# Reordering a kernel's prologue: four slab reads behind the last store, table work ahead of filter copies, a late constant

## The chip, the cores and the metric

The kernel runs on one core of a Trainium2 chip. The metric is device time per execution in microseconds (us), and a kernel's time is the median of its executions. Every profile shown here is one execution of the program, taken by the hardware profiler; times in it count from the start of its span, which is about 1.75 us shorter than the device time of the same execution.

## The reference, cut to what matters

```python
def _attn_ref(x, filt_r, filt_i):            # x: (8, 3008, 256)
    X = np.fft.rfft(x, axis=1)
    Y = X * (filt_r + 1j * filt_i)[None]     # filters: (1505, 256)
    return np.fft.irfft(Y, n=3008, axis=1)

def _moe_ref(x, w_gate, w_val, w_out):       # (24064, 256), d_ff 1536
    return (np.maximum(x @ w_gate, 0) * (x @ w_val)) @ w_out
```

## The kernel before

A spectral filter feeds a gated feed-forward. The transform of one batch goes in two steps. The first (psA) makes four slabs, which are stored to a DRAM buffer (Abuf) and read back in another order (at). The second (psX) multiplies the slabs by tables; its result is multiplied by the filters (tt and uu), transformed back (psD, Dbuf, dC, psY) and then used by the main stream: gate and value products (psG, psV), VectorE's product of the two, output products (psO). Batches from the second on are transformed between main-stream steps. Batch 0 has to be done before the main stream can begin: this is the prologue, about 60 us, and the change is in it.

```python
def load_at(b, c):                     # slab c back from DRAM, 768 rows of 512 B
    ...
    nc.sync.dma_start(ats[b][c:c + 125:4], _ap(Abuf[b], ...))
def make_back_t(q):                    # back table, PE then VectorE
    ...
        nc.vector.tensor_copy(I2t[:, 8 * q + e:8 * q + 8:2, :], psI[e])
def make_back_u(q):                    # second table out of the first
    nc.tensor.matmul(psI, swap, I2t[:, 8 * q:8 * q + 8, :], start=True, stop=True)
    nc.scalar.copy(I2u[:, 8 * q:8 * q + 8, :], psI)
def place_filter(fi, a, half, copy):   # 32 filter rows to their second place
    copy(dst[r + 32:r + 64, gs, :], dst[r:r + 32, gs, :])
def warm(n, cols=512):                 # filler matmuls on junk, to keep the clock up
    ...
# prologue
    load_x(0, nc.sync, ...)            # batch 0, 3 MB
    nc.sync.dma_start(WF, ...)         # fold table, first used for batch 2
    ...                                # filters: GpSimd's queue
    for i, f in enumerate(items_a(0)): # 16 psA items; every fourth ends in a store
        f()
        if i == 12:
            load_at(0, 0)
            load_at(0, 1)
    for c in range(2, 4):
        load_at(0, c)
    ...                                # filter copies, tables: see the diff
    for i in range(15):
        warm(2)
    load_x(1, nc.sync, ...)            # next batch, 3 MB
    first_b(amid)                      # psX, products, inverse of batch 0
```

In the timelines here the fillers and psX, and VectorE's filter copies and table evictions, run in the order in which the program gives them. In the profile before, psX starts at 36.16 us, as the last filler ends, and VectorE's first table eviction at 25.99 us, behind three filter copies that had waited for their rows until 23.06 us. So a filler that runs too long delays psX, and a waiting filter copy delays the tables.

Of the kernel before, what the change touches and what calls it, by code (L numbers as in the profile page):

```python
# [35 lines left out]
def _ap(t, offset_elems, ap_list):  # L36
    return dataclasses.replace(
        t, offset=t.offset + offset_elems, ap=[list(p) for p in ap_list]
    )
# [81 lines left out]
def kernel(  # L121
# [10 lines left out]
    nc = tc.nc  # L132
# [11 lines left out]
    wa_h, fold_h, f2_h, tab_h = _tables()  # L144
# [14 lines left out]
    WF = consts.tile([128, 4, 32], FP32)  # L159
# [11 lines left out]
    def load_x(b, eng, cols):  # L171
        w = NX2 * D
        for c, c0, c1 in cols:
            for m in range(3):
                rows = min(32, B * N1 - (b * N1 + 32 * m))
                eng.dma_start(XF[c][m:m + 4 * rows - 3:4, c0:c1],
                              _ap(x, (b * N1 + 32 * m) * N2 * D + c * w + c0,
                                  [[N2 * D, rows], [1, c1 - c0]]))
# [20 lines left out]
    def make_back_u(q):  # L199

        psI = ps.tile([128, 8, 64], FP32, tag=fft_tag(), name="psI")
        nc.tensor.matmul(psI, swap, I2t[:, 8 * q:8 * q + 8, :], start=True, stop=True)
        nc.scalar.copy(I2u[:, 8 * q:8 * q + 8, :], psI)

    def place_own():

        for i, t in enumerate((I2t, I2u)):
            o = 192 + i * 128
            nc.vector.tensor_copy(t[64:, NG - 2:, :],
                                  tabs[64:, o:o + 128].rearrange("p (g n) -> p g n", g=2))  # L210
        nc.vector.tensor_copy(M1, tabs[:NROW, 448:])
# [21 lines left out]
    def place_filter(fi, a, half, copy):  # L233

        dst = FILT[fi][1]
        gs = slice(H * half, H * half + H)
        r = a * 64
        copy(dst[r + 32:r + 64, gs, :], dst[r:r + 32, gs, :])

    def place_nyq():  # L240
        for (src, dst), n in zip(FILT, nyq):
            nc.vector.tensor_copy(dst[96:97, NG - 1, :], n)
# [20 lines left out]
    def fft_tag(side=False):  # L263
        if side and turn.get("side"):
            return turn["side"]
        turn["i"] += 1
        return turn["tags"][turn["i"] % len(turn["tags"])]

    def items_a(b):

        def one(c, j, st):
            if j == 0:
                st["asb"] = sb.tile([128, NC2 * D], BF16, tag="asb", bufs=4, name="asb")
            psA = ps.tile([128, 512], FP32, tag=fft_tag(True), name="psA")
            o = (c * NC2 % NX2) * D + j * 512
            nc.tensor.matmul(psA[0:NROW], WA, XF[c * NC2 // NX2][:, o:o + 512],
                             start=True, stop=True)
            dst = st["asb"][:NROW, j * 512:(j + 1) * 512]
            nc.scalar.copy(dst, psA[0:NROW])
            if j == 3:  # L280
                eng = nc.scalar if b and c > 1 else nc.sync
                eng.dma_start(_ap(Abuf[b], c * NROW * NC2 * D, [[NC2 * D, NROW], [1, NC2 * D]]),
                                  st["asb"][:NROW])
        for c in range(N2 // NC2):
            st = {}
            for j in range(NC2 * D // 512):
                yield lambda c=c, j=j, st=st: one(c, j, st)
# [59 lines left out]
    def load_at(b, c):  # L347
        if c == 0:
            ats[b] = sb.tile([128, NG, D], BF16, tag="at", bufs=1, name="at")
        nc.sync.dma_start(ats[b][c:c + 125:4],  # L350
                          _ap(Abuf[b], c * NROW * NC2 * D, [[D, 32], [4 * NC2 * D, NG], [1, D]]))
# [164 lines left out]
    def warm(n, cols=512):  # L516

        psJ = ps.tile([128, 512], FP32, tag=fft_tag(True), name="psJ")
        for i in range(n):
            nc.tensor.matmul(psJ[:, :cols], junk[:, 0:128], junk[:, :cols], start=True, stop=True)  # L520
# [12 lines left out]
    nc.vector.memset(XF[1][:, 0:2 * q], 0.0)  # L533
    nc.gpsimd.memset(XF[1][:, 2 * q:], 0.0)
    load_x(0, nc.sync, ((0, 0, q), (0, q, 2 * q), (0, 2 * q, 4 * q), (1, 0, 2 * q), (1, 2 * q, 4 * q)))
    nc.sync.dma_start(WF, nc.inline_tensor(fold_h, name="dft_fold").ap())
    for (src, dst) in FILT:
        nc.vector.memset(dst[64:128, NG - 2:, :], 0.0)
    load_own_filters()
# [4 lines left out]
    warm(11)  # L544
    for i, f in enumerate(items_a(0)):
        f()
        if i == 12:
            load_at(0, 0)
            load_at(0, 1)
    for c in range(2, 4):  # L550
        load_at(0, c)
    for half in range(2):
        for a in range(2):
            place_filter(0, a, half, nc.vector.tensor_copy)
    for i in range(3):
        make_back_t(i)
    warm(6)
    place_filter(1, 0, 0, nc.vector.tensor_copy)
    for i in range(3):
        make_back_u(i)  # L560
    place_own()
    for a, half in ((1, 0), (0, 1), (1, 1)):
        place_filter(1, a, half, nc.vector.tensor_copy)
    place_nyq()
    for i in range(15):
        warm(2)
    load_x(1, nc.sync, ((0, 0, 2 * q), (0, 2 * q, 4 * q), (1, 0, 4 * q)))

    early = items_a(1)

# [116 lines left out]
```

## Time and profile before

| what | value |
|---|---|
| time before, first three executions | 895.17 to 895.47 us, median 895.28 |
| the profiled execution | 896.64 us (span 894.9) |
| TensorE busy | 97% of the span |
| first forward product psX | 36.16 us |
| first product of the main stream (VectorE) | 63.63 us |

The lines themselves are in the prediction.

### The profile page before, as it was taken

What the parts mean: (1) busy time and instruction counts of PE and PEld (TensorE: products, weight loads), DVE (VectorE), ACT (ScalarE), POOL (GpSimd) and SP (SyncE); (2) the same over time, 40 slices, a digit from 0 to 9 for tenths busy, and PEclk for the clock granted to TensorE, in tenths of its full rate; (3) what the DMA queues carried; (4) which work ended last, traced back from release to release, by engine and by line L of the source; (5) the groups of instructions that cost most, each with busy time, mean ns of one, the idle gap of its engine ahead of it and who ended that gap; (6) DMA issues with size and microseconds to landing.
All of it is one profiled execution on the core that took longest, in us unless ns stands there. A gap on an engine that the chain in (4) does not pass through costs nothing.

```text
span 894.9 us, 19039 instructions
## 1 busy us (share of the span) xinstructions
PE 871.8 (97%) x7090; PEld 508.0 (57%) x7210; DVE 569.0 (64%) x873; ACT 499.4 (56%) x891; POOL 364.6 (41%) x361
## 2 busy tenths in 40 slices
PE   8899999999999999999999999999999999999997
PEld 2335555556556565556655565556655566666665
DVE  2737766577665776667765677657766577655553
ACT  4375565556555556555655565555565555555553
POOL 4350698038661386415672167802867000000001
PEclk9999999999999999999999999999999999999999
DMA  8997448534465335463365333763446512331111
GB/s 246 288 224 164 135 132 176 113 96 116 123 156 135 113 101 140 129 144 92 100 172 136 97 100 105 181 139 79 115 140 149 120 31 81 82 73 36 37 32 53
DMA packets 114099, 109.18 MB, mean 122 GB/s; under 512 B 20359, under 2 KB 98599, under 8 KB 113366
## 3 DMA queue, kind: packets, MB, share of 16 engines
q1 hardware_dynamic: 90294, 80.10, 34.8%
q0 software_dynamic: 22992, 26.41, 12.1%
q8 instruction: 57, 0.93, 0.5%
q10 hardware_dynamic: 720, 1.45, 0.4%
q14 instruction: 36, 0.29, 0.1%
HBM read 61.93 MB, written 49.81 MB: 125 GB/s over the span
## 4 chain that ended last, share of the span: by engine, by line
PE 85%; DVE 4%; ACT 4%; DMA 3%; issue 1%; POOL 1%; SPq 1%; POOLq 0%; ACTq 0%; DVEq 0%
PE psG L467 26%; PE psO L486 25%; PE psV L467 24%; DVE prod L472 3%; PE psF L323 3%; ACT vsb L470 3%; PE psD L394 2%; PE psX L364 2%; PE psY L451 2%; DMA at<-Abuf 1%; DMA Fti<-in_filt_i_dram 1%; PE psJ L520 1%; SPq L340 1%; ACT dsb L401 0%; DMA XF<-in_x_dram 0%
## 5 line engine op out<-in xcount | busy, mean ns | idle before, releaser
L472 DVE SCALAR_TENSOR_TENSOR prod<-psG,vsb 128x512 bf16<-128x512 f32 x564 | 388.8, 690 | 263.7 <-ACT vsb L470 257.8
L470 ACT CAST vsb<-psV 128x512 bf16<-128x512 f32 x564 | 332.1, 589 | 263.9 <-PE psV L467 180.3
L467 PE MATMUL psG<-yT,WgT 128*128 128x512 bf16 x1107 | 330.7, 379 | 6.9 <-DVE prod L472 0.8
L486 PE MATMUL psO<-WoT,prod 128*128 128x256 bf16 x2256 | 336.4, 273 | 1.1
L467 PE MATMUL psV<-yT,WvT 128*128 128x512 bf16 x1030 | 315.2, 380 | 0.8 <-ACT asb L330 0.5
L486 PEld LDWEIGHTS <-prod 128*128 128x128 bf16 x2256 | 220.6, 98 | 143.4
L467 PEld LDWEIGHTS <-WgT 128*128 128x128 bf16 x1128 | 110.0, 98 | 136.2 <-issue 3.3
L467 PEld LDWEIGHTS <-WvT 128*128 128x128 bf16 x1128 | 98.6, 98 | 41.8 <-issue 30.5
L258 POOL CAST scr<-prod 128x8 f32<-128x8 bf16 x24 | 4.6, 191 | 258.8 <-DVE prod L472 258.8
L509 POOL DMA_DIRECT2D out_dram<-osb x5 | 2.6, 536 | 195.9 <-ACT osb L499 195.9
L380 DVE TENSOR_TENSOR tt<-psX,Ftr 128x512 bf16<-128x512 f32 x96 | 65.0, 681 | 7.9 <-PE psX L364 7.9
L499 ACT COPY osb<-psO 128x512 f32<-128x512 f32 x92 | 53.9, 586 | 27.9 <-PE psO L486 27.3
L309 POOL TENSOR_TENSOR fold<-XP 128x1024 f32<-128x1024 f32 x24 | 56.5, 2356 | 20.5 <-PE psF L323 19.4
L380 DVE TENSOR_TENSOR uu<-psX,Fti 128x512 bf16<-128x512 f32 x89 | 60.4, 679 | 0.0
L401 ACT CAST dsb<-psD 128x512 bf16<-128x512 f32 x96 | 51.5, 589 | 12.1 <-PE psD L394 11.7
L296 POOL DMA_DIRECT2D XP<-in_x_dram x96 | 56.7, 596 | 3.2 <-PE psG L467 1.6
L310 POOL TENSOR_TENSOR XP<-XP 128x1024 f32<-128x1024 f32 x24 | 56.4, 2350 | 1.9
L330 ACT CAST asb<-psF 128x512 bf16<-128x512 f32 x48 | 25.8, 589 | 30.5 <-PE psF L323 30.5
L330 DVE CAST asb<-psF 128x512 bf16<-128x512 f32 x48 | 30.9, 686 | 18.6 <-PE psF L323 17.0
L456 ACT CAST yT<-psY 128x512 bf16<-128x512 f32 x47 | 27.6, 586 | 22.9 <-PE psY L451 22.7
L458 DVE CAST yT<-psY 128x512 bf16<-128x512 f32 x47 | 32.0, 680 | 9.8 <-PE psY L451 9.8
L451 PE MATMUL psY<-M,dC 96*128 96x94 bf16 (+18 forms) x604 | 37.5, 198 | 0.6 <-DMA dC<-Dbuf 0.5
(70 smaller groups left out, 494.0 us busy)
## 6 DMA issues: line engine op xcount, KB each, us to landing
at<-Abuf SPq DMA_DIRECT2D x32, 384.0 KB
dC<-Dbuf SPq DMA_DIRECT2D x64, 192.0 KB
XP<-in_x_dram POOLq DMA_DIRECT2D x48, 256.0 KB, 5.9
Dbuf<-dsb SPq DMA_DIRECT2D x23, 512.0 KB
XP<-in_x_dram POOLq DMA_DIRECT2D x96, 96.0 KB, 2.7
Abuf<-asb SPq DMA_DIRECT2D x96, 96.0 KB
out_dram<-osb SPq DMA_DIRECT2D x69, 94.0 KB
XF<-in_x_dram SPq DMA_DIRECT2D x15, 256.0 KB
```

Source lines behind the costliest of these rows:

```text
L296: nc.gpsimd.dma_start(xp[r:r + 24, 0:4:2, :], _ap(x, (b * N1 * N2 + o) * D, [[N2 * D, 24], [47 * N2 * D, 2], [1, 512]]))
L309: tt(t, xp[:, 0:2], xp[:, 2:4], op=ALU.add)
L310: tt(xp[:, 2:4], xp[:, 0:2], xp[:, 2:4], op=ALU.subtract)
L330: copy(asf[:, :, q, :], banks[q])
L380: nc.vector.tensor_tensor(p, psX, filt, op=ALU.mult)
L401: nc.scalar.copy(dsb[:, a, o:o + 2, :], psD[a])
L451: nc.tensor.matmul(psY[:, o:o + w], dCs[b, n2 // 8][:, n2 % 8, h * 128:(h + 1) * 128], M1[:, n1:n1 + w], start=True, stop=True)
L467: nc.tensor.matmul(pt[:, :W], w[:, h, ft * 128:(ft + 1) * 128], yt[:, h, :], start=(h == 0), stop=(h == 1))
L470: nc.scalar.copy(vsb, psV[:, :W])
L472: nc.vector.scalar_tensor_tensor(prod, in0=psG[:, :W], scalar=0.0, in1=vsb, op0=ALU.max, op1=ALU.mult)
L486: nc.tensor.matmul(psO[:, t % 2], prods[ft][:, t * 128:(t + 1) * 128], WoT[:, ft, :], start=(ft == 0), stop=(ft == NFT - 1))
L499: copy(osb[:, t0 % 2:t % 2 + 1], psO[:, t0 % 2:t % 2 + 1])
```

## The change

The intent is to have batch 0's slabs in SBUF sooner. Store 3 is to go out before any slab read, so that the last read can follow it earlier; the back tables are to be made before VectorE turns to filter copies that wait for transfers; ScalarE takes two of these copies; the fold table, needed much later, gives up its early place.

```diff
     load_x(0, nc.sync, ((0, 0, q), ...))
-    nc.sync.dma_start(WF, nc.inline_tensor(fold_h, name="dft_fold").ap())
...
     for i, f in enumerate(items_a(0)):
         f()
-        if i == 12:
-            load_at(0, 0)
-            load_at(0, 1)
-    for c in range(2, 4):
+    for c in range(4):
         load_at(0, c)
-    for half in range(2):
-        for a in range(2):
-            place_filter(0, a, half, nc.vector.tensor_copy)
     for i in range(3):
         make_back_t(i)
     warm(6)
-    place_filter(1, 0, 0, nc.vector.tensor_copy)
+    place_filter(0, 1, 0, nc.scalar.copy)
     for i in range(3):
         make_back_u(i)
+    for a, half in ((0, 0), (0, 1), (1, 1)):
+        place_filter(0, a, half, nc.vector.tensor_copy)
     place_own()
-    for a, half in ((1, 0), (0, 1), (1, 1)):
-        place_filter(1, a, half, nc.vector.tensor_copy)
+    for a, half, copy in ((1, 0, nc.scalar.copy), (0, 0, nc.vector.tensor_copy),
+                          (0, 1, nc.vector.tensor_copy), (1, 1, nc.vector.tensor_copy)):
+        place_filter(1, a, half, copy)
     place_nyq()
-    for i in range(15):
+    for i in range(14):
         warm(2)
     load_x(1, nc.sync, ...)
+    nc.sync.dma_start(WF, nc.inline_tensor(fold_h, name="dft_fold").ap())
```

## The prediction

> **What bounds the kernel now.** I read the page first: the busy shares and the chain that ended last.
>
> ```profile
> PE 871.8 (97%) x7090; PEld 508.0 (57%) x7210; DVE 569.0 (64%) x873; ACT 499.4 (56%) x891; POOL 364.6 (41%) x361
> ...
> PE 85%; DVE 4%; ACT 4%; DMA 3%; issue 1%; POOL 1%; SPq 1%; POOLq 0%; ACTq 0%; DVEq 0%
> ```
>
> TensorE is busy for 97% of the span and carries 85% of the chain. In order of time, the main stream (gate, value and output products) begins near 61.6 us and hardly pauses afterwards. The diff touches nothing of it: TensorE's instruction list differs only by two dropped filler matmuls in the prologue. So the change can move the time only by shifting the start of that stream, and everything is decided in the first 60 us. What the forward products of batch 0 (psX) wait for is the next view, the timeline of TensorE (start us, length us, engine, line, operation):
>
> ```profile
> 26.80 0.39 PE L202 MATMUL psI<-I2t,tabs 128*128 128x512 bf16 x1 [2.12 <-DVE I2t L197]
> 27.46 1.25 PE L202 MATMUL psI<-I2t,tabs 128*128 128x512 bf16 x2 [0.27 <-DVE I2t L197]
> 28.50 7.74 PE L520 MATMUL psJ<-junk 128*128 128x512 bf16 x30
> 36.16 0.41 PE L364 MATMUL psX<-at,F 64*64 64x256 bf16 x8
> ```
>
> Thirty filler matmuls run from 28.50 to 36.16 us and psX follows without a gap. Filler is meant to fill a wait; here it was itself the last thing waited for. The timeline of GpSimd, whose small copy reads all four slabs, says when the data was there:
>
> ```profile
> 35.16 0.18 POOL L258 CAST scr<-at 32x8 f32<-32x8 bf16 x1 [18.73 <-DMA at<-Abuf]
> ```
>
> The last slab landed by 35.16 us, so the filler cost 1.0 us. It ran late for two reasons. It stands behind the back tables, whose VectorE copies (25.99 us) stood behind four filter copies that waited for filter transfers. And the granted clock was 0.50 from 28 to 30 us (the stretches view): 30 matmuls took 7.74 us instead of the 6.5 us that 0.216 us each at full clock would give (the main stream's spacing: 0.43 us for two).
>
> Second, the slabs. The SyncE queue's timeline, and its waits (us in total, times, longest):
>
> ```profile
> 21.03 2.98 SPq L350 DMA_DIRECT2D at<-Abuf  x2
> 24.10 0.79 SPq L282 DMA_DIRECT2D Abuf<-asb  x1
> 26.32 5.84 SPq L350 DMA_DIRECT2D at<-Abuf  x2
> ```
>
> ```profile
> SPq L350 <- DMA Abuf<-asb: 8.5, 4, 4.6
> ```
>
> Each slab read waits for its own store to land. Store 3 is issued at 24.10 us, behind two reads, and read 3 waits 4.6 us for it, to 31.59 us. What the DMA engines did meanwhile is in their busy row for 32 to 34 us (40 slices of 0.05 us):
>
> ```profile
> DMA  0000000000000000000445698999877563689999
> ...
> DMA packets 489, 0.25 MB, mean 125 GB/s; under 512 B 1, under 2 KB 489, under 8 KB 489
> ```
>
> They were empty for nearly 1 us from 32 us. Counting packet time on the engines per microsecond, the idle part was about 0.58 us in 31 to 32, 0.96 us in 32 to 33 and 0.18 us in 33 to 34, together 1.7 us. From 17 to 31 us they are full. So the slabs' arrival is bound by DMA work plus this hole.
>
> **What the Trainium skill says.** "DMA: Bandwidth & Descriptors", section "Queues, rings and completion order": descriptors of one queue are consumed in ring order on each engine, and an engine takes turns between queues. The trace agrees: reads 0 and 1 are issued from 21.03 us, but their 512-byte packets appear only from 25.5 us, behind stores 1 and 2, in turn with the filters' packets of GpSimd's queue. Section "Anatomy of one DMA — SWDGE (gpsimd) path" puts most of the roughly 2 us fixed cost of a transfer into the receipt of the write; here store 3's last 4 KB packets run before 31 us and the queue is released at 31.59 us, which fits a smaller receipt. "TensorE: Matmul & The Clock Gate", Part 1: after an idle window of about 3.4 us the clock falls to half; the trace has one such window at half, 27.3 to 30.7 us, after 3.4 us in which TensorE was busy for about 1.2 us. "ScalarE: Activation LUTs", "Rules for kernel authors": about 0.3 us plus 0.83 ns per element, hence an estimated 2.85 us for a filter copy of 3072 elements on ScalarE, against 0.95 us on VectorE in this trace. No ScalarE copy of that size is in the trace to check it with; its 512-element ones take 0.58 us, slightly below the page's sum of 0.72.
>
> **The change part by part.**
>
> Slab reads behind store 3. The evictions of store 3's data end at 23.23 us, so it is issued at about 23.3 instead of 24.10. What matters more is the ring: reads 0 and 1 (768 packets of 512 bytes each at about 28 ns over 16 engines = 1.34 us each) no longer stand before it. It follows store 2, whose packets end at 25.5 us. Store 3 is 96 packets of 4 KB at 165 ns over 16 engines = 1.0 us of service; in turn with the filters, which last to about 28 us, nearer 2 us. It should land at about 28.3 us. By then three reads, 4.0 us of service, are queued, so read 3, issued at about 29 us, joins a full ring and the hole goes: -1.7 us.
>
> Fold table last. Its 64 KB come as 512-byte packets of 40 ns (112 were seen): 112 x 40 / 16 = 0.28 us less ahead of the slabs: -0.3 us. In its new place it is 0.3 us behind 3 MB of the next batch, and first used hundreds of microseconds later: 0. Its 0.6 us of issue on SyncE falls at about 35 us, where that queue idles until the first Dbuf store (44.70 before): 0.
>
> The last slab therefore lands at 35.1 - 1.7 - 0.3 = 33.1 us.
>
> Tables first. psI for them is ready from 22.54 to 23.28 us, the six VectorE copies take 2.08 us, so they end at about 25.3 instead of 28.07. Six fillers end at 24.7, the three table products at about 25.6, and 28 fillers x 0.216 = 6.0 us at full clock end at about 31.6. With TensorE nearly without a gap from 23.9 to 27.3 us the half-clock window of before should not come there. The filler is then off the path, and psX starts at about 33.2 us instead of 36.16: -2.9 us, of which 2.0 belong to the slabs and 0.9 to the filler.
>
> Filter copies. VectorE: tables to 25.3, three Ftr copies x 0.95 to 28.2, three small ones x 0.2 to 28.8, three Fti copies to 31.7, two Nyquist rows to 32.1. ScalarE: first copy 23.3 to 26.1 (its rows landed at 23.06), three table evictions to 28.0, second copy from 28.2 to 28.9 (the landing of Fti) to about 31.5. Both are ready before 33.2, by 1 us and more: 0 on the path.
>
> Afterwards psX, products, inverse, Dbuf stores and dC reads form a chain of engine and transfer lengths, 36.16 to 61.6 us, whose parts are unchanged; the next batch's 3 MB move earlier along with read 3. I expect it to shift as a whole. Nearly all of the 2.9 us should reach the end, as the main stream has no slack that waits for a fixed time. I take off 0.1 us for a clock loss described next. Sum: 895.28 - 2.8 = 892.5 us.
>
> **The rivals.** First, the clock falls later. TensorE now idles from about 31.6 to 33.2 us. In the window 30.7 to 34.1 us it would be busy about 0.9 us of filler plus 0.9 us of the first products, half of it; 35% was too little before, 67% (37.5 to 41) enough. A half-clock window from 34.1 would lengthen psX and fillers, but products there wait mostly for GpSimd's uu and VectorE, so 0.3 to 1 us: a time near 893.3. Chance about a third.
>
> Second, filters replace slabs. Store 3's 4 KB packets, in turn with the filters' 0.5 KB ones, delay the last filter rows by up to 0.8 us; if ScalarE's copy is slower too, the first uu waits until perhaps 33.5 to 34 us: a time of 893 to 893.5. For it: margins of 1 us only. Against: VectorE loses two of eight copies and the tables come first.
>
> Third, the hole does not close: store 3 crawls beside the filters and read 3 still arrives on an empty ring. Then only the filler's 1 us and the 0.3 us of the table remain: 894 us. Against: 4 us of reads stand behind store 3.
>
> Fourth, a larger gain: fillers were cut from 30 to 28, as if the slabs were expected by about 31.6 us. If stores land sooner with less queued, psX at 32.2 gives 891.4.
>
> **Range and chances.** The gain lies in the prologue and can hardly exceed 4.5 us or turn into a loss of over 1 us; 2% is 17.9 us. Range 891.2 to 894.0. Faster by over 2%: 0.01; within: 0.98; slower: 0.01.
>
> **What would show it.** Right: reads all after store 3 on the SyncE queue; the wait for it ending near 28.5; no empty DMA slices between 31 and 33 us; last slab landed near 33.1; filler over near 31.6, with no half clock at 28 to 30; psX near 33.2; the main stream 2.8 us earlier. Wrong: psX held by filler again, a product held by a filter copy on ScalarE, DMA idle before read 3, or a shift of psX that the Dbuf and dC transfers swallow.

## The result, and the profile after

The changed kernel took 894.21 us, the median of four executions from 893.26 to 895.10; the kernel before took 895.38 us in four. The ratio is 0.9987, with a 95% interval of 0.9970 to 1.0004. (A ratio is the mean time of one kernel's fast runs over that of the other's of the same rounds, so not quite the ratio of the medians.) The forecast was 892.5 us with a range up to 894.0. The medians moved in the forecast direction, by 1.2 us where 2.8 were forecast; this interval still includes no change; of the changed kernel's three, only that of the third call below does not. A difference within 2% had been given a chance of 0.98, and by that measure all runs count as the same.

The page's busy shares and chain of the changed kernel:

```profile
PE 875.7 (98%) x7208; PEld 506.8 (57%) x7208; DVE 567.1 (64%) x871; ACT 504.2 (57%) x893; POOL 364.4 (41%) x361
...
PE 93%; DMA 3%; ACT 1%; POOL 1%; issue 1%; DVE 0%; SPq 0%; ACTq 0%; POOLq 0%
```

TensorE carries 93% of the chain, against 85% before. TensorE's timeline where before the filler led straight into psX:

```profile
25.24 0.91 PE L202 MATMUL psI<-I2t,tabs 128*128 128x512 bf16 x3
25.99 6.21 PE L520 MATMUL psJ<-junk 128*128 128x512 bf16 x28
34.34 0.41 PE L364 MATMUL psX<-at,F 64*64 64x256 bf16 x8 [2.14 <-DMA at<-Abuf]
```

The table products come at once, without the waits for VectorE of before. The 28 fillers run at full clock and are over at 32.2 us, and psX waits 2.14 us for slabs. So the filler is off the path, but the slabs land at 34.3 us and not at 33.1. ("Land" here means the moment at which the waiting engine is released; the last packet runs about 0.6 us earlier.) The SyncE queue's timeline, its wait for stores (us in total, times, longest), and the DMA busy row of 30 to 32 us (40 slices of 0.05 us):

```profile
12.63 11.65 SPq L282 DMA_DIRECT2D Abuf<-asb  x4
24.37 5.68 SPq L350 DMA_DIRECT2D at<-Abuf  x4
```

```profile
SPq L350 <- DMA Abuf<-asb: 3.0, 2, 1.8
```

```profile
DMA  9999999888666553466789999998865789999999
```

All four reads stand behind all four stores, the longest wait for a store fell from 4.6 to 1.8 us, and the empty microsecond has become two dips (30 to 32 us as a whole is 89% busy). The slab part works as designed; it yields less than it was credited with.

The two profiles differ by more than their prologues. The stretch from the main stream's first to its last VectorE product took 820.9 us before and 820.3 after. Each trace has one wait of 0.8 us in it for a transfer that came just too late, in a different place: before, psX for a slab read at 183.7 us; after, psY for a dC read at 570.2 us. Over the fourteen profiles that stretch varies from 819.6 to 821.2 us, though its program is always the same. A difference of 1 us between two single profiles therefore proves nothing about a prologue, and below I read prologues by their own landmarks.

### The profile page after: what moved, and what is told of

Same layout as the page of the kernel before. It is cut to its first block, busy times and chain, and to the rows that moved or that the text cites. A ratio compares the mean times of both kernels' runs of the same rounds, so it can differ in the third digit from the quotient of the medians.

```text
span 892.0 us, 19155 instructions
## 1 busy us (share of the span) xinstructions
PE 875.7 (98%) x7208; PEld 506.8 (57%) x7208; DVE 567.1 (64%) x871; ACT 504.2 (57%) x893; POOL 364.4 (41%) x361
## 4 chain that ended last, share of the span: by engine, by line
PE 93%; DMA 3%; ACT 1%; POOL 1%; issue 1%; DVE 0%; SPq 0%; ACTq 0%; POOLq 0%
PE psV L467 28%; PE psG L467 27%; PE psO L486 27%; PE psF L323 3%; PE psY L451 2%; PE psD L394 2%; PE psX L364 2%; PE psA L276 2%; DMA dC<-Dbuf 1%; DMA Abuf<-asb 1%; DMA at<-Abuf 1%; DMA XF<-in_x_dram 1%; ACT dsb L401 0%; DMA Dbuf<-dsb 0%; SPq L176 0%
## 5 line engine op out<-in xcount | busy, mean ns | idle before, releaser
L467 PE MATMUL psV<-yT,WvT 128*128 128x512 bf16 x1128 | 336.6, 380 | 0.7 <-ACT asb L330 0.4
L467 PE MATMUL psG<-yT,WgT 128*128 128x512 bf16 x1128 | 335.4, 379 | 0.7 <-ACT dsb L401 0.3
```

What stands on the lines that cost most here:

```text
L467: nc.tensor.matmul(pt[:, :W], w[:, h, ft * 128:(ft + 1) * 128], yt[:, h, :], start=(h == 0), stop=(h == 1))
```

## The experiments

Runs of one call share a chip and the executions of the kernel before, which ranged from 894.14 to 899.34 us in the first call, 894.26 to 897.32 in the second and 894.11 to 896.50 in the third. All gave correct results.

### The kernel before, once more

No edit. What was expected:

> The kernel before once more, with a second profile. The profiled execution of before took 896.64 us, its timed ones 895.2 to 895.6. If that is because only the profiled one had the half-clock window in its filler (27.3 to 30.7 us), this profile, where it takes about 895.3 us, has filler at full clock, over at about 35.1 us, and psX within 0.3 us of the slabs; then the filler was never worth 0.9 us in timed runs. If the filler usually binds, psX is again 0.8 us or more behind the slabs. Time 895.2 to 895.6 by both.

It took 895.24 us (894.36 to 898.24), the kernel before beside it 894.88. Its profiled execution took 894.87 us with a granted clock of 1.000. TensorE's timeline of it:

```profile
26.37 0.39 PE L202 MATMUL psI<-I2t,tabs 128*128 128x512 bf16 x1 [1.33 <-DVE I2t L197]
...
27.91 6.63 PE L520 MATMUL psJ<-junk 128*128 128x512 bf16 x30
35.44 0.41 PE L364 MATMUL psX<-at,F 64*64 64x256 bf16 x8 [0.90 <-PE psJ L520]
```

This is the same program as in the prediction's fence, and it tells another story. The 30 fillers took 6.63 us instead of 7.74, were over at 34.5 us, and psX came 0.9 us later, when the slabs landed. (The view names psJ as releaser, but psJ had long ended; the slab copy on GpSimd shows what arrived.)

```profile
35.47 0.18 POOL L258 CAST scr<-at 32x8 f32<-32x8 bf16 x1 [18.66 <-DMA at<-Abuf]
```

In the kernel before, the filler binds where a half-clock window falls on it. This part of the forecast gain, 0.9 us, was read from an execution of the slower kind.

### The changed kernel again, and with a longer filler

The first is unchanged; the "bridge" makes the filler reach to the slabs:

```diff
-    for i in range(14):
+    for i in range(18):
         warm(2)
```

> The changed kernel once more, for its spread. Theory clock (the filler-free gap of 2.1 us before psX lets the clock fall to half in some executions, by the phase of its windows): times in two groups, about 893.4 and about 894.8, the longer ones with a granted clock of 0.996 to 0.997, the shorter with 0.998 to 0.999. Theory late transfers (waits of about 1 us on slab or dC reads later in the main stream, in any execution): the same spread, but no tie between time and clock. Median 893.5 to 894.5 by both.

> The changed kernel with 18 pairs of fillers in place of 14, over at about 34.0 us, just before the slabs. Theory clock: no gap, so no half-clock window later; all executions near 893.4 us, clock 0.998 or more, spread under 0.6 us: median 0.5 to 0.8 us under the changed kernel's. Theory late transfers: spread and median as the changed kernel's. If the slabs land before 34 us in some executions, the filler costs up to 0.5 us.

The changed kernel took 894.19 us (893.42 to 898.17), the bridge 893.51 us (892.75 to 895.56), the kernel before 894.88. Ratios to before: 0.9993 (0.9972 to 1.0014) and 0.9980 (0.9963 to 0.9998). All six executions of the changed kernel had a clock of 0.998; those of the bridge had 0.999 or 1.000. The changed kernel's second profile shows where the clock fell. Its table of stretches, with the granted clock third from the end:

```profile
30.00:34.00 4.00, 1.93 (x9) 0.69 (x7) 1.97 (x4) 0.82 (x1) 0.00 (x0) 1.00 0.99 301
34.00:38.00 4.00, 3.81 (x32) 1.96 (x36) 3.17 (x5) 1.28 (x3) 2.42 (x4) 0.58 1.02 348
```

The half-clock window lies at 34.6 to 38.0 us, on the first psX and fillers. The slabs of this profile landed, by GpSimd's copy, at:

```profile
34.22 0.18 POOL L258 CAST scr<-at 32x8 f32<-32x8 bf16 x1 [17.30 <-DMA at<-Abuf]
```

In the bridge's profile TensorE idles only 0.66 us:

```profile
25.40 7.93 PE L520 MATMUL psJ<-junk 128*128 128x512 bf16 x36
33.99 0.41 PE L364 MATMUL psX<-at,F 64*64 64x256 bf16 x8 [0.66 <-PE psJ L520]
```

So the gap in front of psX does pull the clock down, which was the prediction's first rival. But its cost does not stand out in the stretch behind it: from psX to the first main-stream product of VectorE it is 27.58 us here and 27.44 in the third call's profile of the changed kernel, both with the window, and 27.30 to 27.73 in the ten profiles without one behind psX (27.35 in the changed kernel's first, 27.32 and 27.69 in the bridge's two). What was called the theory of the clock (two groups 1.4 us apart) is therefore wrong in size, and my expectation of the bridge's spread failed too: it still scatters by 2.8 us at full clock. The 898.17 us execution has the same clock as the 893.42 one. What delays such executions is not settled; they occur in the kernel before as well (899.34 us).

Both were run again in the third call:

> The changed kernel beside the bridge and the filler-free-change variant in the same rounds, since single executions scatter by over 1 us. If the gap costs a half-clock window nearly every time, clock 0.998 or less in most executions and a profile with a half-clock window that begins within 4 us after psX; median 0.3 to 0.7 us above the bridge of the same call.

> The bridge (18 pairs of fillers) again: clock 0.999 to 1.0 in most executions, no half-clock window near psX in the profile, psX at 34.0 to 34.4 us, median 0.3 to 0.7 us under the changed kernel of the same call.

The changed kernel took 893.94 us, the bridge 893.62, before 895.27 (ratios 0.9985, interval 0.9972 to 0.9997, and 0.9980, 0.9966 to 0.9993). Clocks were 0.997 to 0.999 and 0.999 to 1.000; the changed kernel's profile has its half-clock window at 33.9 to 37.3 us. The difference between the two, 0.3 us after 0.7 in the first call, is near the lower end of what was expected, and no interval for it was measured.

### One part of the change at a time

"Slabs only" is the kernel before with the four reads behind the last store:

```diff
-        if i == 12:
-            load_at(0, 0)
-            load_at(0, 1)
-    for c in range(2, 4):
+    for c in range(4):
         load_at(0, c)
```

> The kernel before with only the slab reads moved behind the last store; tables, fillers and fold table as before. Slabs land near 34.3 us, but 30 fillers end at 35.0 us at full clock and near 36.1 with the half-clock window: so by both theories nearly nothing, 895.0 to 895.4 us (0 to 0.3 less), as filler takes the place of the slabs. If it shows 894.2 or less, the filler is not what binds and the slab reads carry the whole change.

It took 894.50 us against 894.88 (ratio 0.9985, 0.9968 to 1.0003). In its profile read 3 is issued at 29.84 us, fillers are over at 34.15 us, and psX comes at 34.92, released by the slabs:

```profile
27.51 6.64 PE L520 MATMUL psJ<-junk 128*128 128x512 bf16 x30
34.92 0.41 PE L364 MATMUL psX<-at,F 64*64 64x256 bf16 x8 [0.78 <-DMA at<-Abuf]
```

That is 0.5 us before the second profile of the kernel before: more than the expected nearly nothing, and under half of the 1.1 to 1.4 us by which the changed kernel's psX moved. In time the two can't be told apart: the changed kernel's ratio of this call, 0.9993, is even the higher one.

"Fold table only" moves that one load behind the next batch's reads:

```diff
-    nc.sync.dma_start(WF, nc.inline_tensor(fold_h, name="dft_fold").ap())   # behind batch 0's reads
...
     load_x(1, nc.sync, ...)
+    nc.sync.dma_start(WF, nc.inline_tensor(fold_h, name="dft_fold").ap())
```

> The kernel before with only the fold table moved behind the next batch's reads. By packet time (128 of 40 ns on 16 engines) the slabs should land 0.3 us earlier, at about 35.1 us, still after the filler: 894.6 to 895.0 us, 0.3 less than before. If the place on the ring counts for more (store 0 is issued 0.65 us earlier), up to 0.6 us less.

psX came at 35.13 us, 0.3 us before the 35.44 of the kernel before at full clock, as the packet sum said:

```profile
35.13 0.41 PE L364 MATMUL psX<-at,F 64*64 64x256 bf16 x8 [0.93 <-PE psJ L520]
```

But this proves little. GpSimd's slab copy came at 35.16 us here, and at 35.16, 35.47 and 35.64 us in the three other profiles in which the slab reads and the fold table stand as before: one program scatters by as much as the effect. The time, 895.71 us with one execution of 900.70 (ratio 1.0013, 0.9992 to 1.0034), can't show 0.3 us either. Nor do the parts add up: alone they moved psX by 0.5 and 0.3 us, together, with filler out of the way, by 1.1 to 1.5. Both moves together are measured here, the share of each is not.

"Tables only" keeps reads, fold table and 30 fillers and takes the new order of tables and filter copies:

```diff
-    for half in range(2):
-        for a in range(2):
-            place_filter(0, a, half, nc.vector.tensor_copy)
     for i in range(3):
         make_back_t(i)
     warm(6)
...                                    # the rest as in the change
```

> The kernel before with only the back tables ahead of the filter copies and two of those on ScalarE (slab reads, fold table and 30 fillers as before). Theory slabs (in an execution without the half-clock window the slabs at 35.4 us bind, the filler was over at 34.4): fillers over near 32.3 us, psX still at 35.4, no gain, and a gap of 3 us, so a half-clock window after it in most executions (clock 0.998): 895.0 to 895.5 us. Theory of the prediction (filler worth 0.9 us): 894.0 to 894.3.

It took 895.02 us against 895.22 (ratio 0.9999, 0.9986 to 1.0012). Its fillers were over at 32.45 us, and psX waited until 35.62 us, when the slabs landed:

```profile
25.81 6.64 PE L520 MATMUL psJ<-junk 128*128 128x512 bf16 x30
35.62 0.41 PE L364 MATMUL psX<-at,F 64*64 64x256 bf16 x8 [3.17 <-issue]
```

Without the slab part there is no gain, as the slab theory said. This gap of 3.17 us brought no half-clock window in the profile, though three of the five executions had a clock under 0.999, at 894.9 to 896.5 us. Two of those have a clock of 0.996, too low for a single window. That stays open.

"Slabs and fold table" joins both moves and leaves the old table order. It ran in the second call and again in the third:

> Slab reads behind the last store and fold table last, but tables, copies and 30 fillers as before: the changed kernel without its filler part. If the slabs alone carry the change, psX comes at 34.2 to 34.5 us as in the changed kernel, held for 0.2 us at most by filler that ends at about 34.2; with no gap there is no half-clock window (clock 0.999 to 1.0), so 893.5 to 894.1 us, as fast as the changed kernel or faster. If the tables ahead matter, 894.5 or more.

> Slab reads and fold table moved, old table order and 30 fillers, again. Its first profile had psX at 33.91 us and 892.98 us, but its five timed executions 895.8 to 897.8. If the old table order lets a half-clock window into the fillers in most executions (they then end near 35.2 us), times near 894.3 with clock 0.998. If the first call was only disturbed, about 893.3 to 893.8 with clock 0.999. If 896 or more comes again, something in it that neither theory names.

The medians were 896.22 us (before: 895.22) and 895.52 us (before: 895.27), so no gain, though its two profiled executions took 892.98 and 895.61 us. Their TensorE timelines, the second call's and then the third's:

```profile
25.72 0.39 PE L202 MATMUL psI<-I2t,tabs 128*128 128x512 bf16 x1 [1.03 <-DVE I2t L197]
...
27.26 6.64 PE L520 MATMUL psJ<-junk 128*128 128x512 bf16 x30
33.91 0.41 PE L364 MATMUL psX<-at,F 64*64 64x256 bf16 x8
```

```profile
26.48 0.39 PE L202 MATMUL psI<-I2t,tabs 128*128 128x512 bf16 x1 [1.96 <-DVE I2t L197]
...
28.18 7.73 PE L520 MATMUL psJ<-junk 128*128 128x512 bf16 x30
35.85 0.41 PE L364 MATMUL psX<-at,F 64*64 64x256 bf16 x8
```

One program, two executions, 1.9 us apart at psX. In both, the slabs had landed by 34.2 us. In the second, TensorE waited longer for the tables (VectorE's filter copies got their rows at 22.74 us, against 21.98 in the first), the clock was 0.50 from 27 to 30 us, and the fillers held psX until 35.85 us. This is the state in which the kernel before was profiled. In this kernel it seems to be usual: nine of its eleven executions had a clock under 0.999, with a median of 895.97 us; the other two have 893.44. It does not follow from the old table order alone: the kernel before had such a clock in 10 of 37 executions and slabs only in one of six. Why both moves together bring it on is not shown. So the table part earns nothing by itself; beside both moves it takes the filler out of the way, and their gain is no longer lost in most executions. The expectations had only part of this; the second call's times, up to 897.77 us, are higher than the filler explains.

Put together by granted clock: it is given to three decimals, and one window of 3.4 us costs about 0.002. Most traces also have a half-clock stretch at their end, after the last matmuls, of up to 2.5 us; it costs up to 0.0014, so that 0.999 and 1.000 both mean no window in the work itself. The table has the executions of all three calls and the changed kernel's first four, outliers included, so only large differences count:

| kernel | clock 0.999 or more: executions, median us | below: executions, median us |
|---|---|---|
| before | 27, 894.88 | 10, 896.20 |
| changed | 2, 893.88 | 13, 893.94 |
| bridge | 11, 893.62 | none |
| slabs and fold table | 2, 893.44 | 9, 895.97 |

A window goes with about 1.3 us in the kernel before. In the changed one, where the profiles have it behind the start of psX, 13 executions with it and two without it have the same median; two are too few for more than that.

### Why the slabs land at 34.2 us and not at 33.1

> A measurement, slower on purpose perhaps: the changed kernel with a small store of slab data ahead of the next batch's nine reads on the SyncE queue, so that they are issued only after the slabs landed. In the changed kernel about 1.3 us of those reads' packets run on the engines before the last slab packet. If they take time from the slabs (contention), the slabs now land about 1 us earlier, near 33.2 us. If they only fill engines that are already done with their own share of the slabs (uneven rings), the slabs land as before, near 34.2. The time may rise by up to 1 us as the first product of batch 1 waits for its data.

```diff
+    gate = dram.tile([4, D], BF16, name="gate")
+    nc.sync.dma_start(gate, ats[0][0:4, NG - 1, :])
     load_x(1, nc.sync, ...)
```

The reads of the next batch were then issued from 35.16 us, none of them ahead of the slabs. The slabs landed at 34.85 us, as GpSimd's copy shows:

```profile
34.85 0.18 POOL L258 CAST scr<-at 32x8 f32<-32x8 bf16 x1 [17.66 <-DMA at<-Abuf]
```

That is later, as the whole execution was: read 3 was issued at 30.07 us and not at 29.29. From its issue to the last slab packet it took 4.2 us, and 4.3 us in the changed kernel's second profile. So, in the one profile that tests it, the next batch's packets take no time from the slabs. The rest was mispredicted: the median rose to 898.44 us, 3.2 over the kernel before (ratio 1.0037, 1.0018 to 1.0055), as the first psA of batch 1 waited 3.1 us for its data and the clock fell twice.

The account of the missing part, from the packets of two profiles (kernel before at full clock, changed kernel's second): before, engines were idle for 0.84 + 0.97 + 0.46 = 2.3 us between 31 and 34 us. The change removes this hole. But 1.0 us of engine time, against 0.2, now goes to packets of the next batch that run before the last slab packet. Since these cost the slabs nothing, I infer that they ran on engines that were through with their own slab packets while others were not. So 2.3 - 0.8 = 1.5 us were to be had, and the last slab packet moved from 34.88 to 33.61 us, by 1.3. The prediction had divided the work evenly by 16. The same shows at read 3: it is issued 2.5 us earlier (29.29 and not 31.80 us), but from its issue to the last slab packet it takes 4.3 us instead of 3.1. (All profiles with the reads as before have 3.0 to 3.1 us here; those with the new order, the split filters below left out, have 4.2 to 4.6.) That the rings, the engines' shares of the queue, are unequally filled is inferred; the traces do not say which engine ran a packet.

### Filters in two halves

From the finding that slabs wait behind queued work, I tried to take work out of their way: the second half of each filter is loaded after the first slab read has landed, and copied between product steps.

```diff
-    for _ in filters:
-        pass
+    next(filters)                       # first halves only
...
+    hold_gpsimd(ats[0][0:1, NG - 1, 0:8])
+    for _ in filters:                   # second halves
+        pass
...
     def amid(i):
+        if i == 1 or i == 2:
+            for a in range(2):
+                place_filter(i - 1, a, 1, nc.vector.tensor_copy)
...                                    # 12 pairs of fillers; Nyquist rows later; of the
                                       # first-half copies two change engines
```

> Follows from the finding that the slabs' arrival is bound by the work queued on the DMA engines: the filters' second half (needed only from the fourth product step on) is loaded after the first slab read has landed, and copied between product steps; 24 fillers. About 4 us of filter packets leave the time before the slabs: psX near 31 to 32 us in place of 34.2. If the later filter copies on VectorE fit into its waits, the time falls to about 891 to 892.5; if they and the later loads hold up the products, the gain is lost and it stays at 893.5 to 895.

It took 901.95 us (ratio 1.0073, 1.0060 to 1.0085). Its chain in order of time (start us, us, what):

```profile
30.78 12.65 DMA Fti<-in_filt_i_dram
43.43 0.02 issue
43.46 1.59 DVE Fti L251
```

The late filter rows landed only at 43.4 us, among the next batch and the weights, and held VectorE and the products. Nor did psX gain: it came at 33.77 us and not at 31 to 32. Store 3 is issued at 23.38 us, within the 23.1 to 24.0 of the other profiles with this order of reads; the DMA engines were now 80% idle from 23 to 24 us; and the four reads alone are 5.4 us of packet time, from 25.4 us on. The finding that slabs are bound by queued work held only as far as that.

## Why the prediction was wrong, point by point

**What bounds the kernel.** Right: only the start of the main stream moves. It left out that the main stream itself varies by up to 1.6 us between executions.

Two terms of the sum failed: the filler, of which -0.9 us was expected, and the slabs, of which -2.0.

**The filler cost 1.0 us.** This step failed first. It was true of the one profiled execution. In the second profile, at full clock, the slabs bound psX by 0.9 us and the filler cost nothing; by their clocks, 27 of 37 executions were of this kind. The profiled execution's 896.64 us against 895.3 was the warning. Of the 2.9 us forecast for psX, 36.16 is the wrong start; against 35.44 the changed kernel's profiles (34.34, 34.19, 34.06) gain 1.1 to 1.4 us. So 0.7 us of the forecast was lost at the start, and 0.9 to 1.1 us at the end, where 33.2 was forecast.

**Slab reads behind store 3, -1.7 us.** Right in mechanism, off in size: the hole closed and read 3 was issued at 29.3 us (forecast 29), but slab and fold table parts together moved the landing by 1.25 us (35.47 to 34.22) and not by 2.0. About 0.8 us of the hole went to packets of the next batch instead; that uneven rings are the reason is inferred.

**Fold table last, -0.3 us.** Not contradicted and not shown: psX came 0.3 us earlier with that part alone, but the landing scatters by 0.5 us over three profiles in which neither slab reads nor fold table were changed (35.16 to 35.64).

**Tables first.** Right: fillers over at 31.8 to 32.2 us (forecast 31.6), at full clock. Its worth is not a fixed 0.9 us but depends on the execution.

**Filter copies off the path.** Right. ScalarE's copies took 2.75 us, the second from 29.25 to 32.0 us; VectorE was done at 32.3. (The estimate was 2.85 us. Its source, "ScalarE: Activation LUTs" of the Trainium skill, "Rules for kernel authors", gives the 0.3 us for an instruction whose bias is a pointer operand, which the prediction left out.) All this is 2 us before psX needs it, so the second rival falls.

**The rest shifts as a whole.** Right: 27.45 and 27.47 us from psX to the first main-stream product before, 27.35 to 27.58 after.

**The rivals.** The first, a clock that falls later, was given a third and came, by the granted clock, in 13 of 15 executions; its cost of 0.3 to 1 us did not stand out behind psX, and the bridge, which has no such window, was 0.7 and 0.3 us faster by its medians. The third (hole stays) and the fourth (larger gain) did not come.

**Small readings.** The first packets of the slab reads appear at 25.1 us in the profile before, not 25.5, and TensorE was busy for 65% from 37.5 to 41 us, not 67%. Neither matters to the sum.

Worked out anew: about -1.25 us for the slabs, nothing for the filler, and for the clock not more than the 0.3 to 0.7 us of the bridge's medians, for which there is no interval. Measured differences of medians: -1.2, -0.7 and -1.3 us in three sets of executions. The bridge, with four more pairs of fillers, is the fastest kernel seen by its medians, about 1.4 us and 1.7 us under the kernel before, and beats the kernel before clear of noise.

## What to carry to other kernels

Compare the time of the profiled execution with the timed ones before reading a wait from it: a wait that depends on when the clock falls is in some executions and not in others, and a second profile is the cheapest experiment. A filler sized to fill a wait must end just before the awaited data in the execution with the slow clock as well as in the fast one, or stand where a half-clock window does no harm. When a hole in the transfers is closed, the whole of it need not come back: here 1.3 of 2.3 us did, probably because the last packet is on the fullest ring and not on the average one.

## What the Trainium skill lacked or had wrong

- "TensorE: Matmul & The Clock Gate", Part 1, lets the clock fall after an idle window of about 3.4 us and advises against idle gaps longer than that. Gaps of 2.0 to 2.6 us sufficed here in five profiles, while gaps of 2.1 and 3.2 us (the changed kernel's first profile, tables only) brought no half clock. The share of a window decides, counted in windows of 3.4 us from the clock records of each trace: at full clock, windows in which TensorE was busy for 34 to 39% (1.1 to 1.3 us) were followed by one at half clock in these five profiles; windows of 51 and 56% (tables only, around its gap) and of 42% (slabs only, at its end) were not. The page gives no such share.
- The same page says that the phase of the windows varies from run to run and puts the cost of the ramp under 1% of a span. The runs show that it can decide whether a change of 1 us is seen: 33.91 or 35.85 us at psX for one program, 1.1 us of it in slower fillers.
- "DMA: Bandwidth & Descriptors", "Anatomy of one DMA — SWDGE (gpsimd) path": about 2 us of fixed cost, mostly receipt, for GpSimd's path; the section has no figure for SyncE's. There it was about 0.6 us from the last packet to the release of the waiting engine, for store 3 (28.69 to 29.29 us) and for the slabs (33.61 to 34.22 us).
- No page has how much of a gap between transfers comes back when it is closed: here 1.3 of 2.3 us at the last slab packet, while 1.0 us of engine time went to later transfers before it.
